# Turning q and k of two prologue steps in row halves: 64 tokens by 128 channels a product, with two heads side by side

## The chip, the core and the metric

The kernel runs on one core of a Trainium2 chip. The metric is the device time of one execution in microseconds; the time of the kernel before is the median of 7 executions. Trace times below are counted from the start of the profiled span.

## What is computed

Retention (attention with a decaying state) over 4 batches, 8 heads, 768 tokens and 64 channels a head, followed by a two-layer block with a quick GELU:

```python
for t in range(S):
    state = gamma * state + einsum('bhd,bhe->bhde', k[:, :, t], v[:, :, t])
    y[:, :, t] = scale * einsum('bhd,bhde->bhe', q[:, :, t], state)
x = y.transpose(0, 2, 1, 3).reshape(B * S, H * D)      # 3072 x 512
h = x @ w_in                                            # 512 x 2048
out = (h * sigmoid(1.702 * h)) @ w_out                  # 2048 x 512
```

All results are float32; w_in and w_out arrive as float64 and are narrowed on the chip.

## The kernel before

The sequence is cut into 24 steps. Step j takes 64 tokens of two batches: batch half i lies on partitions 64i to 64i+63, so that a loaded tile is 128 tokens (half i, token t) by 8 heads by 64 channels. Heads are paired as s and s+4 (s from 0 to 3, r is 0 or 1 for the lower or upper of the pair). In the turned tiles qT and kT a partition is (r, channel), and the free axis is (s, half i, token).

Four steps make a block of 512 tokens for the two-layer block. Steps 0 to 7, blocks 0 and 1, belong to a prologue that also fetches and narrows the weights. Later steps are loaded in squares of 32 and turned by VectorE; the change does not touch them.

For a prologue step j the work is:

- `load` (L114): q, k and v come in through SyncE's queue (SP) with one DMA for each batch half and tensor, issued at L126. A tile has two buffers, so step j's load waits until step j-2's tile is read out. Each DMA on that queue also waits on one of eight semaphores taken in turn, so for the landing of the DMA issued eight before it.
- `turn` (L222): TensorE turns q and k by products with the identity (L232). For k, then q, 16 products in all: 128 tokens by 64 channels stand in the array, 128 columns of the identity stream through, and the result goes to partition half r of a PSUM tile `pt`. There is one `pt` tile for q and one for k, of 2 KB a partition each.
- `turned` (L240): ScalarE copies `pt` of k and of q to kT and qT (L243), 128 by 512 each. These lie in G in a place that depends on j being even or odd, so that step 6's copy of q waits until step 4 has read its own.
- `decay` (L245): ScalarE scales k by head into `kd` with eight small instructions (L254).
- `attend` (L258): TensorE makes the scores of step j from kT and qT (L265), and for an earlier step f the state's update from kd and v (L275), the part of the output from the old state (L284) and the part from the masked scores and v (L290). `masked` (L294) on VectorE multiplies the scores by the decay mask (L296).

The weights come in 32 pieces ("w5a" and so on, `fetch`, L163) on the same SP queue. Narrowing one of 15 larger units is an ACT instruction (`abs`, L189) and six VectorE instructions (`half`, L193 to L195, and `rest`, L199 to L204). `up0` and `up1` (L384, L396) are the products of the first layer for blocks 0 and 1, and `gate` and `gated` (L356, L361) apply the GELU.

The prologue's order is written out by hand in one long list of names, which TensorE, ScalarE, VectorE and SP each follow for their own work. Around the two steps concerned it reads:

```python
        ... w5b updated3 v5 decay4 k6 abs1 x3 gated0.0.2 q6 turn5 half1 up0.0.3 turned5 up0.1.2 step4
        aged4 w5a rest1 v4 gate0.0.3 decay5 w6a masked4 turn6 gate0.1.2 abs5 w6b step5-4 gated0.0.3 half5
        rest5 up0.0.1 updated4 turned6 k7 abs6 gated0.1.2 ... w4b ... w8a ... w4a q7 ... step6-5 w8b half4
        gate0.1.5 state5 updated5 turn7 turned7 aged6 abs8 w9b up0.1.6 ... step7-6
```

`step5-4` is `attend` with j = 5 and f = 4. After the prologue the main loop runs the second layer of blocks 0 and 1 and both layers of blocks 2 to 5, on TensorE in the order of the code.

Of the kernel before, what the change touches and what calls it, by code (L numbers as in the profile page):

```python
# [9 lines left out]
F32 = mybir.dt.float32  # L10
U32 = mybir.dt.uint32
AF = mybir.ActivationFunctionType
ALU = mybir.AluOpType
P = 128
# [14 lines left out]
def kernel(  # L29
# [29 lines left out]
    pe, act, dve, pool, sp = nc.tensor, nc.scalar, nc.vector, nc.gpsimd, nc.sync  # L59
    ctx.enter_context(tc.manual_schedule(engines={mybir.EngineType.PE}))  # L60

    B, H, S, D = q.shape
    NT, DM = out.shape
    DFF = moe_w_in.shape[1]
    HP = H // 2
    NC = S // D
    NCH = B // 2 * NC
    CB = 4
# [13 lines left out]
    ps = ctx.enter_context(tc.tile_pool(name="ps", bufs=2, space=bass.MemoryType.PSUM))  # L82
# [10 lines left out]
    G = const.tile([P, NP, 4, TH], F32, name="G")  # L93
# [7 lines left out]
    ident = const.tile([P, P], F32, name="ident")  # L101
# [6 lines left out]
    def pin(i):  # L108
        return tc.keep_in_program_order(i) if ordered[0] else i


    QKV = {}

    def load(j, what="qkv"):  # L114

        b, c = j // NC * 2, j % NC
        rows = slice(c * D, (c + 1) * D)
        keep = tc.keep_in_program_order if j < 2 * CB else lambda i: i  # L120

        def plain(name, src, tag, bufs, engine=sp):
            t = two.tile([P, H, D], F32, name=name + "_in", tag=tag, bufs=bufs)
            QKV[name, j] = t
            for i in range(2):
                keep(engine.dma_start(t[i * D:(i + 1) * D], src[b + i, :, rows, :].rearrange("h p d -> p h d")))  # L126

        if j < 2 * CB:
            if "q" in what:
                plain("q", q, "q_sq", 2)  # L130
            if "k" in what:
                plain("kn", k, "k_sq", 2, sp if j else act)
        elif "q" in what:
            for name, src in (("q", q), ("k", k)):
                t = two.tile([P, HP, P // C4, C4], F32, name=name + "_sq")
                for r0 in range(0, P, C4):
                    d0, h0 = r0 % D, r0 // D * HP
                    for n in range(P // C4):
                        t0 = c * D + n * C4 % D
                        tc.keep_in_program_order(sp.dma_start(  # L140
                            t[r0:r0 + C4, :, n], src[b + n * C4 // D, h0:h0 + HP, t0:t0 + C4, d0:d0 + C4]
                            .rearrange("h p d -> p h d")))
                QKV[name, j] = t
        if "v" in what:
            if j >= 2 * CB and c < NC - 1:
                plain("kn", k, "kn", 1)
            plain("v", v, "v", 2)
# [61 lines left out]
    QT, KT, KD, AT, TURNED, PA, PU, PY, SHARE = [{} for _ in range(9)]  # L209
    HALF = [slice(i * D, (i + 1) * D) for i in range(2)]  # L210
    TWO = [(i, r) for i in range(2) for r in range(2)]

    def home(j, name):

        at = ["qT", "kT", "kd", "at"].index(name)
        shape = [[HP, P], [HP, P], [H, D], [2, HP, D]][at]
        if j >= 2 * CB:
            return one.tile([P] + shape, F32, name=name, tag=name, bufs=[2, 1, 1, 2][at])
        t = G[:, at, j % 2 * 2:j % 2 * 2 + 2].rearrange("p s t -> p (s t)")
        return t.rearrange("p (a b c) -> p a b c", a=2, b=HP) if at == 3 else t.rearrange("p (a b) -> p a b", a=shape[0])  # L220

    def turn(j):  # L222

        QT[j], KT[j] = home(j, "qT"), home(j, "kT")
        if j < 2 * CB:

            x = QKV.pop(("q", j)), QKV["kn", j]
            TURNED[j] = p = [ps.tile([P, HP, P], F32, name="pt", tag="y") for i in range(2)]
            for n in (1, 0) if j else (0, 1):
                for s in range(HP):  # L230
                    for r in range(2):
                        pe.matmul(p[n][HALF[r], s, :], x[n][:, HP * r + s, :], ident, start=True, stop=True)  # L232
        else:
            for t, name in ((QT[j], "q"), (KT[j], "k")):
                tc.keep_in_program_order(dve.transpose(
                    t.rearrange("p h t -> p (h t)"), QKV.pop((name, j)).rearrange("p h s d -> p (h s d)")))
        if 2 * CB <= j < NCH - 2:
            load(j + 2, "qk")

    def turned(j):  # L240
        p = TURNED.pop(j)
        for n in (1, 0) if j else (0, 1):
            pin(act.activation((QT[j], KT[j])[n], p[n], AF.Copy))  # L243

    def decay(j):  # L245

        if j % NC == NC - 1:
            return
        KD[j] = home(j, "kd")
        x, d = QKV["kn", j], cold[:, H:2 * H, None]  # L250
        if j < 2 * CB:

            for h in range(H):
                pin(act.activation(KD[j][:, h], x[:, h], AF.Copy, scale=d[:, h]))  # L254
        else:
            pool.tensor_mul(KD[j], x, d.to_broadcast([P, H, D]))  # L256

# [76 lines left out]
    def step(j, f=None):  # L334
        attend(j, f)
        if j is not None:
            masked(j)
            if j > 2 * CB:
                decay(j)
        if f is not None:  # L340
            c = f % NC
            if c == 0:
                updated(f)
            else:
                by_state(f)
            output(f)
            if 0 < c < NC - 1:
                aged(f)
                updated(f)
        if j is not None and 2 * CB < j < NCH - 1:  # L350
            load(j + 1, "v")
# [227 lines left out]
    def late_loads():  # L579
        load(2 * CB, "qkv")  # L580
        load(2 * CB + 1, "qk")
# [9 lines left out]
    for j in range(2 * CB):  # L591
        for name in "qkv":
            works[f"{name}{j}"] = lambda j=j, name=name: load(j, name)
        works |= {f"{name}{j}": lambda j=j, do=do: do(j) for name, do in (
            ("turn", turn), ("turned", turned), ("decay", decay), ("masked", masked), ("state", by_state),
            ("x", output), ("aged", aged), ("updated", updated))}
        for f in (None, *range(2 * CB)):
            works[f"step{j}" + ("" if f is None else f"-{f}")] = lambda j=j, f=f: attend(j, f)
        works[f"step-{j}"] = lambda j=j: attend(None, j)
    for i in range(2 * NFF):  # L600
        works[f"w{i // 2}{'ab'[i % 2]}"] = lambda i=i: fetch(i)
    for name, i in [("0a", 0), ("0b", 1)] + [(str(p), 2 * p) for p in range(1, NFF)]:
        n = Narrow(i)
# [48 lines left out]
    def chunks(first, last):  # L652

        return [s for j in range(first, last + 1)
                for s in (lambda j=j: turn(j), lambda j=j: step(j, j - 1))]

    for m in range(NB):
        between = []
        if m == 0:
            between = [lambda: turn(2 * CB), lambda: step(2 * CB), lambda: None, lambda: None, lambda: turn(2 * CB + 1)]  # L660
        elif m == 1:
            between = [lambda: (decay(2 * CB), load(2 * CB + 1, "v"))] + chunks(2 * CB + 1, 3 * CB)[1:]
        elif 1 < m < NB - 2:
            between = chunks((m + 1) * CB + 1, (m + 2) * CB)
        elif m == NB - 2:
            between = chunks((m + 1) * CB + 1, NCH - 1) + [lambda: step(None, NCH - 1)]
        if m > 1:
            for d in range(NP // 2):
                up(d)
        for n, unit in enumerate(down(m)):  # L670
            unit()
            if m == 0 and n < NP and n % 2:
                sums_w2(n - 1)
            if m == 0 and NP <= n < 3 * NP // 2:
                sums_w2_t3(2 * (n - NP))
            if m == 1 and n % 8 == 3:
                sums_w1(n // 4)
            if between and n % 3 == 2:
                between.pop(0)()
                if m and not between:  # L680
                    sums_x()
# [46 lines left out]
```

## Time and profile before

| | us |
|---|---|
| median of 7 executions | 685.87 (682.03 to 686.83) |
| the profiled execution | 685.87 |
| its span, first to last instruction | 683.9 |
| TensorE busy (PE) | 672.7 |
| weight loads busy (PEld) | 560.6 |
| VectorE busy (DVE) | 367.0 |
| ScalarE busy (ACT) | 150.8 |
| GpSimd busy (POOL) | 125.5 |

In the profile, PE is a TensorE product and PEld the load of its standing operand; a float32 product appears as two records of each. SPq is the time in which SP issues a DMA, which lands later. The granted TensorE clock was 1.00 throughout. The turns of steps 6 and 7 begin at 51.24 us and 71.20 us. The span's 683.9 us and the execution's 685.87 us differ by about 2 us that lie outside the traced instructions.

### The profile page before, as it was taken

What the parts mean: (1) busy time and instruction counts of PE and PEld (TensorE: products, weight loads), DVE (VectorE), ACT (ScalarE), POOL (GpSimd) and SP (SyncE); (2) the same over time, 40 slices, a digit from 0 to 9 for tenths busy, and PEclk for the clock granted to TensorE, in tenths of its full rate; (3) what the DMA queues carried; (4) which work ended last, traced back from release to release, by engine and by line L of the source; (5) the groups of instructions that cost most, each with busy time, mean ns of one, the idle gap of its engine ahead of it and who ended that gap; (6) DMA issues with size and microseconds to landing.
All of it is one profiled execution on the core that took longest, in us unless ns stands there. A gap on an engine that the chain in (4) does not pass through costs nothing.

```text
span 683.9 us, 13882 instructions
## 1 busy us (share of the span) xinstructions
PE 672.7 (98%) x5830; PEld 560.6 (82%) x5830; DVE 367.0 (54%) x514; ACT 150.8 (22%) x293; POOL 125.5 (18%) x116
## 2 busy tenths in 40 slices
PE   6999999999999999999999999999999999999997
PEld 3888854747888888888888888888888888888886
DVE  3899994989810843443652453563445372345241
ACT  4775423321000001332000332000333000233000
POOL 3000000000367414000335000244100243000030
PEclk9999999999999999999999999999999999999999
DMA  7886641322222223300323310323310220000001
GB/s 185 218 218 217 186 140 62 123 81 35 49 34 68 58 46 89 71 4 13 73 49 85 61 34 9 72 31 88 74 40 3 46 48 32 16 0 1 16 0 47
DMA packets 140334, 46.55 MB, mean 68 GB/s; under 512 B 131824, under 2 KB 132848, under 8 KB 140272
## 3 DMA queue, kind: packets, MB, share of 16 engines
q1 hardware_dynamic: 136352, 39.10, 24.8%
q0 software_dynamic: 1760, 5.26, 2.0%
q10 hardware_dynamic: 2160, 1.31, 0.6%
q8 instruction: 46, 0.75, 0.5%
q14 instruction: 16, 0.13, 0.1%
HBM read 39.33 MB, written 6.29 MB: 67 GB/s over the span
## 4 chain that ended last, share of the span: by engine, by line
PE 84%; DVE 7%; SPq 4%; DMA 3%; issue 1%; ACT 0%; POOL 0%; ACTq 0%
PE pd L503 37%; PE px L435 16%; PE py L435 12%; PE ph L384 6%; SPq L140 4%; PE ph L396 4%; PE pa L265 2%; PE pt L232 2%; PE py L290 2%; PE py L284 1%; PE pa L275 1%; PE pd L488 1%; DMA whole<-in_col_decay_dram 1%; DMA W<-in_moe_w_out_dram 1%; DVE G L425 1%
## 5 line engine op out<-in xcount | busy, mean ns | idle before, releaser
L503 PE MATMUL pd<-W,G 128*128 128x256 f32 x1088 | 240.5, 381 | 0.6 <-DVE G L426 0.3
L503 PEld LDWEIGHTS pd<-W,G 128*128 128x128 f32 x1088 | 205.2, 190 | 29.7 <-DVE G L426 1.2
L435 PE MATMUL px<-X,W 128*128 128x256 f32 x512 | 119.0, 379 | 0.0
L435 PEld LDWEIGHTS px<-X,W 128*128 128x128 f32 x512 | 97.3, 190 | 13.2
L435 PE MATMUL py<-X,W 128*128 128x256 f32 x384 | 90.7, 379 | 0.0
L435 PEld LDWEIGHTS py<-X,W 128*128 128x128 f32 x384 | 73.0, 190 | 9.9
L384 PE MATMUL ph<-X,W 128*128 128x256 f32 x256 | 57.6, 382 | 0.0
L396 PE MATMUL ph<-W,W 128*128 128x512 f32 x128 | 55.6, 592 | 0.0
L384 PEld LDWEIGHTS ph<-X,W 128*128 128x128 f32 x256 | 48.1, 190 | 8.2 <-issue 1.1
L256 POOL TENSOR_TENSOR kd<-kn_in,cold 128x512 f32<-128x512 f32 x14 | 16.4, 1168 | 189.8 <-PE pa L275 162.1
L396 PEld LDWEIGHTS ph<-W,W 128*128 128x128 f32 x128 | 24.3, 190 | 28.9 <-issue 28.4
L427 POOL TENSOR_TENSOR G<-G 128x512 f32<-128x512 f32 x20 | 29.5, 1482 | 91.8 <-DVE G L426 90.4
L356 ACT ACTIVATE sg<-G 128x512 f32<-128x512 f32 x48 | 30.3, 630 | 51.3 <-DVE G L445 31.0
L361 DVE TENSOR_TENSOR G<-G,sg 128x512 f32<-128x512 f32 x48 | 33.4, 695 | 13.7 <-ACT sg L356 13.7
L296 DVE TENSOR_TENSOR at<-pa,mask 128x512 f32<-128x512 f32 x16 | 11.0, 685 | 54.0 <-PE pa L275 54.0
L324 POOL TENSOR_TENSOR state<-state,whole 128x512 f32<-128x512 f32 x13 | 13.5, 1041 | 127.9 <-DVE state L332 127.6
L503 PE MATMUL pd<-W,W 128*128 128x256 f32 x160 | 35.8, 381 | 0.7 <-DVE W L426 0.7
L503 PEld LDWEIGHTS pd<-W,W 128*128 128x128 f32 x160 | 30.2, 190 | 6.0 <-DVE W L426 1.5
L356 ACT ACTIVATE sg<-ph 128x512 f32<-128x512 f32 x32 | 19.0, 596 | 67.0 <-PE ph L396 30.1
L475 ACT ACTIVATE u<-pd 128x512 f32<-128x512 f32 x6 | 3.6, 597 | 136.2 <-PE pd L503 136.2
L445 DVE TENSOR_TENSOR G<-py,p 128x512 f32<-128x512 f32 x16 | 11.1, 692 | 38.1 <-PE py L435 38.1
L480 POOL DMA_DIRECT2D out_dram<-o x20 | 14.9, 746 | 89.1 <-DVE o L479 89.1
(112 smaller groups left out, 681.0 us busy)
## 6 DMA issues: line engine op xcount, KB each, us to landing
W<-in_moe_w_in_dram SPq DMA_DIRECT2D x12, 512.0 KB, 6.0
v_in<-in_v_dram SPq DMA_DIRECT2D x48, 128.0 KB, 3.3
kn_in<-in_k_dram SPq DMA_DIRECT2D x42, 128.0 KB, 3.2
W<-in_moe_w_out_dram SPq DMA_DIRECT2D x10, 512.0 KB, 4.1
out_dram<-o POOLq DMA_DIRECT2D x20, 256.0 KB, 2.6
q_sq<-in_q_dram SPq DMA_DIRECT2D x256, 16.0 KB, 1.8
k_sq<-in_k_dram SPq DMA_DIRECT2D x256, 16.0 KB, 1.8
G<-in_moe_w_out_dram SPq DMA_DIRECT2D x6, 512.0 KB, 4.0
```

Source lines behind the costliest of these rows:

```text
L140: tc.keep_in_program_order(sp.dma_start(t[r0:r0 + C4, :, n], src[b + n * C4 // D, h0:h0 + HP, t0:t0 + C4, d0:d0 + C4] .rearrange("h p d -> ...
L232: pe.matmul(p[n][HALF[r], s, :], x[n][:, HP * r + s, :], ident, start=True, stop=True)
L256: pool.tensor_mul(KD[j], x, d.to_broadcast([P, H, D]))
L265: pe.matmul(pa[HALF[i], r, 0, s, :], KT[j][HALF[r], s, HALF[i]], QT[j][HALF[r], s, HALF[i]], start=True, stop=True)
L356: pin(act.activation(s, h, AF.Sigmoid, scale=1.702))
L361: pin(dve.tensor_mul(g, h[:, i], s[:, i]))
L384: pe.matmul(h[:, ab], w, X[:, 2 * th + c // 2, c % 2, :], start=(ab == 0 and c == 0), stop=(c == 3), skip_group_check=True)
L396: pe.matmul(h, w, X1[:, c // 2:4:2, c % 2, :], start=(c == 0), stop=(c == 3))
L427: pool.tensor_sub(a[1], a[1], a[0])
L435: pe.matmul(acc[:, u, :], W1[:, 2 * d + u, sa, c, :], X[:, sb, c, :], start=(start and u == 0 and c == 0), stop=(stop and c == 1), skip_gr ...
L480: (pool if m < NB - 1 else act).dma_start(rows[th, e], o)
L503: pe.matmul(p0[:, n, :], g1(m, p, sa)[:, n * P:(n + 1) * P], W2[:, sb, p, :], start=(new and p == 0 and n == 0), stop=(last and p == NP - ...
```

## The change

For steps 6 and 7 (`paired`), q and k are loaded with the heads s and s+4 next to each other: each batch half of each tensor comes in two DMAs, one for each r, of four heads apiece, to every second head place of the tile. `turn` then makes 16 products again, but each takes one batch half: 64 tokens by 128 channels (both heads of a pair) stand in the array, and 64 columns of the identity stream through. The result fills all 128 partitions. The two `pt` tiles now belong to the batch halves, each with k and q. `turned` copies one half a time into both kT and qT. `decay` picks the heads from their new places. v and all other steps stay.

```diff
+    def paired(j):
+
+        return 2 * CB - 2 <= j < 2 * CB
+
@@ load
         def plain(name, src, tag, bufs, engine=sp):
             t = two.tile([P, H, D], F32, name=name + "_in", tag=tag, bufs=bufs)
             QKV[name, j] = t
+            if paired(j) and name != "v":
+                for i in range(2):
+                    for r in range(2):
+                        keep(engine.dma_start(t[i * D:(i + 1) * D, r:H:2],
+                                              src[b + i, r * HP:(r + 1) * HP, rows, :].rearrange("h p d -> p h d")))
+                return
             for i in range(2):
                 keep(engine.dma_start(t[i * D:(i + 1) * D], src[b + i, :, rows, :].rearrange("h p d -> p h d")))
@@ turn
-        if j < 2 * CB:
+        if paired(j):
+
+            x = QKV.pop(("q", j)), QKV["kn", j]
+            TURNED[j] = p = [ps.tile([P, 2, HP, D], F32, name="pt", tag="y") for i in range(2)]
+            for n in (1, 0):
+                for s in range(HP):
+                    for i in range(2):
+                        pe.matmul(p[i][:, n, s, :], x[n][HALF[i], 2 * s:2 * s + 2, :].rearrange("p r d -> p (r d)"),
+                                  ident[HALF[i], HALF[i]], start=True, stop=True)
+        elif j < 2 * CB:
@@ turned
+        if paired(j):
+            t = G[:, 0:2, j % 2 * 2:j % 2 * 2 + 2, :].rearrange("p n a t -> p n (a t)").rearrange(
+                "p n (s t) -> p n s t", s=HP)
+            for i, p in enumerate(TURNED.pop(j)):
+                pin(act.activation(t[:, :, :, HALF[i]], p, AF.Copy))
+            return
@@ decay
             for h in range(H):
-                pin(act.activation(KD[j][:, h], x[:, h], AF.Copy, scale=d[:, h]))
+                at = h % HP * 2 + h // HP if paired(j) else h
+                pin(act.activation(KD[j][:, h], x[:, at], AF.Copy, scale=d[:, h]))
```

## The prediction

> **What bounds the kernel now.** I read the page's busy times and chain first, then TensorE's timeline around step 6's turn, then the durations of the records concerned, then the SP queue's timeline with the landings.
>
> ```profile
> PE 672.7 (98%) x5830; PEld 560.6 (82%) x5830; DVE 367.0 (54%) x514; ACT 150.8 (22%) x293; POOL 125.5 (18%) x116
> ...
> PE 84%; DVE 7%; SPq 4%; DMA 3%; issue 1%; ACT 0%; POOL 0%; ACTq 0%
> ```
>
> TensorE is busy for 672.7 of 683.9 us and makes 84% of the chain that ended last. TensorE time that is saved or added in the prologue therefore moves the end, unless a wait stands right behind it. In the chain view the turns (L232) hold 2% of the span; the two changed ones look like this on TensorE:
>
> ```profile
> 51.24 1.09 PE L232 MATMUL pt<-ident,kn_in 128*64 128x128 f32 x16
> 52.17 1.04 PE L232 MATMUL pt<-ident,q_in 128*64 128x128 f32 x16
> 53.14 0.69 PE L265 MATMUL pa<-G 64*64 64x64 f32 x32
> 53.66 0.65 PE L275 MATMUL pa<-v_in,G 64*64 64x64 f32 x32
> 54.12 0.65 PE L284 MATMUL py<-G,state 64*64 64x64 f32 x32
> 54.59 0.65 PE L290 MATMUL py<-G,v_in 64*64 64x64 f32 x32
> 55.17 0.70 PE L384 MATMUL ph<-X,W 128*128 128x256 f32 x2
> ```
>
> A turn takes 53.14 - 51.24 = 1.90 us (step 7: 71.20 to 73.10, also 1.90). Its 32 records run as 16 pairs, the two r at once, and successive pairs start 109 ns apart in the trace. The 64x64 products that follow run four at once: 32 records from 53.66 to 54.12, eight groups of 58 ns. TensorE doesn't pause anywhere here.
>
> ```profile
> L232 PEld LDWEIGHTS pt<-ident,kn_in x128: 132/137/230, 9.1 to 71.9; 128*64 128x64 f32 x128
> L232 PE MATMUL pt<-ident,kn_in x128: 272/273/473, 9.1 to 72.0; 128*64 128x128 f32 x128
> ```
> ```profile
> L503 PEld LDWEIGHTS pd<-W,G 128*128 128x128 f32 x1088 | 205.2, 190 | 29.7 <-DVE G L426 1.2
> ```
>
> A load of 64 columns takes 137 ns, of 128 columns 190 ns: 53 ns for 64 more columns, so about 107 ns of column time for 128. A product with 128 moving columns takes 273 ns, with 64 218 ns (the L275 records): 55 ns for 64.
>
> ```profile
> 42.70 1.27 SPq L126 DMA_DIRECT2D kn_in<-in_k_dram  x2
> 44.07 2.08 SPq L126 DMA_DIRECT2D q_in<-in_q_dram  x2
> 46.21 0.61 SPq L163 DMA_DIRECT2D G<-in_moe_w_in_dram  x1
> 46.92 1.27 SPq L126 DMA_DIRECT2D v_in<-in_v_dram  x2
> 48.29 1.87 SPq L163 DMA_DIRECT2D W<-in_moe_w_in_dram  x2
> 50.27 1.60 SPq L126 DMA_DIRECT2D kn_in<-in_k_dram  x2
> ```
> ```profile
> DMA to landing us min/median/max: 5.2/5.4/5.7
> ```
> ```profile
> 52.08 1.18 ACT L189 ACTIVATE W<-G 128x1024 f32<-128x1024 f32 x1 [0.76 <-DMA G<-in_moe_w_in_dram]
> 53.16 0.57 ACT L243 ACTIVATE G<-pt 128x512 f32<-128x512 f32 x1
> ```
>
> SP issues k6, q6, w5a, v4, w6a and w6b, k7 almost without a break. The second fence is v4's landing: its second DMA, issued at 47.56, lands at 52.78, and L275 loads from it from 53.60. So v4 has 0.8 us in hand. w5a lands at 52.00, and ScalarE's narrowing step waited for exactly that.
>
> **What the Trainium skill says.** "TensorE: Matmul & The Clock Gate", section "LDWEIGHTS (loading the stationary operand)": a load costs by its columns, P/1.2 ns, not by its rows. The 53 ns between 137 and 190 agree. The same page, "Part 3: Packing small matmuls": products in different row groups of the array overlap, and so do their loads. The 58 ns for four 64x64 products with their loads agree; a 64x128 pair no run here shows yet. "TensorEngine Tiling (Array Packing)", "Gotcha 1: PSUM Pressure": row tiles must not write one PSUM bank at the same time. Each half has its own 2 KB `pt` tile, so this adds no wait.
>
> **The change part by part.**
>
> *Products.* Removed from each turn: 16 pairs of 109 ns, 1.74 us, which with the two changes of array layout makes the 1.90. Added: 16 pairs of row halves, each with 64 moving columns but 128 standing ones. The streaming alone needs 58 ns a pair, 16 x 58 = 0.93 us (-0.82 us a turn). The load needs 107 ns in each row half; if both halves load at once and behind the running product, a pair costs 107 to 109 ns, 1.74 us (0). If the halves had to load one after the other, a pair costs 214 ns, 3.42 us (+1.68). I take 0: the 64x64 rows show four loads of 53 ns going on within 58 ns, so row halves do load side by side, and nothing in them shows a load faster than its columns. Low end -0.82, high end +1.68 a turn.
>
> *Loads.* SP issues 4 DMAs of 256 short rows for k and q each instead of 2 of 512: 8 more in all, 4 ahead of w5a and v4. An issue of 512 rows takes 0.63 us; the later issues at L140 with 128 rows take 0.43 us. Between them I put 256 rows at 0.50 us (estimate). k6 and q6 then take 2 x (4 x 0.50 - 2 x 0.63) = +1.5 us. q6's first issue took 1.4 us in the trace, 0.8 us of it blocked by transfers still in flight, which smaller DMAs partly avoid: +0.7. Against that, the third and fourth q6 DMA now wait for the eighth DMA before them, v5, which lands at 46.20 and 46.52: q6 ends near 47.2 instead of 46.16, +1.05 us. w5a, v4 and w6 follow by as much. Bounds: 0 (all hidden in the blocked time) and +2.6 us (4 more at 0.63).
>
> *Behind v4.* v4's second half lands at 52.78 + 1.05 = 53.83 instead of 52.78; the third L275 product needs it at 53.62. TensorE waits 0.2 us, with L284, L290 and `up0.0.1` queued behind. At the high end 1.8 us; at the low end 0.
>
> *Behind w5a.* ScalarE's `abs5` and VectorE's half5 start 1.05 us later, and VectorE is then filled up to 88 us. TensorE's first consumer with little room is L265 of step6-5 at 69.18, which needs `masked5` off PSUM at 68.0: 1.15 us in hand, 1.35 with the 0.2 above. Cost 0. The next tight one, `up0.0.7` at 97.42, has 0.9 us in hand behind rest7 (96.52), but VectorE idles 0.63 us at 89.46 and absorbs the rest. If this cover were gone, the excess over it would be TensorE idle.
>
> *Turn waits.* q6 itself lands near 51 us, the q products start at 52.1: 0. The four DMA waits of each tensor sit on the first two products of it; they have fired before. In turn 7 both PSUM tiles are needed at the start, 0.9 us earlier than q's tile before. It is freed by VectorE at about 69.9, 1.0 later 70.9, wanted at 71.2: 0.
>
> *Copies and decay.* Two copies of 512 elements as before, 0.60 us each. Each half now holds k and q, so none can start at mid-turn. In step 6 the second copy waited for L284 anyway (to 54.90); now both do, done by 56.1, before `abs6` at 57.60. In step 7 they run from 73.2 to 74.4, before step7-6 at 76.75; ScalarE's queue behind (aged6, abs8) has finished by 76.7, when the gate's product ends. Decay: the same eight instructions. 0. The built program's order on all engines is otherwise unchanged.
>
> *Sum.* 2 x 0 (turns) + 0.2 (v4) = +0.2 us on the profiled execution of 685.87, which is also the median of the runs: 686.1.
>
> **Rivals.**
>
> *Streaming bound.* The row halves load faster than I read. Turn 6's 0.82 us is given back waiting for v4 (53.83 against 52.8). Turn 7's stays, less some 0.2 us at VectorE-bound consumers near 100 us: 0.2 - 0.82 + 0.2 = -0.4, 685.5; with the loads hidden -1.6, 684.2. For it: the product work is halved. Against it: the 53 ns a 64 columns.
>
> *Late loads.* The issues take 0.63 us each whatever their size: v4 lands 2.6 us later, TensorE waits 1.8 us, 687.7. For it: 0.60 to 0.63 even of 512 rows after any gap. Against it: 0.43 for 128 rows.
>
> *Loads in turn (the slow side).* Both row halves' 128-column loads use one path into the array: 32 x 107 = 3.42 us a turn, at L232 in both steps. v4's lateness hides in it. 2 x 1.68 = +3.4, 689.2. It decides as soon as a pair starts more than 109 ns after the last. For it: no 64x128 product is in the trace. Against it: the 64x64 groups, which also use both row halves.
>
> **Numbers.** A measurement can tell about 0.3%, 2.06 us, from no change; the runs of before alone spread from 682.03 to 686.83. Chances: forecast 0.60, streaming bound 0.20, late loads 0.10, loads in turn 0.10. The range takes in both ends of the unknown costs except the last case: 684.2 (-1.6) to 688.0 (+1.8 and a little). Faster by over 0.3% only comes from the streaming case plus scatter: 0.10. Slower: 0.10 from loads in turn, 0.04 from late loads, 0.04 from scatter: 0.18. Within: 0.72.
>
> **What would show it.** In the new timeline, pairs of L232 at 128x64 columns for steps 6 and 7 start 109 ns apart (58: streaming bound; 214: loads in turn), and the turn takes about 1.9 us. v4 is issued near 48.0 and lands near 53.8; TensorE pauses about 0.2 us before L275 of step5-4. `abs5` starts near 53.1. It is wrong if a turn is shorter than 1.5 us or longer than 2.3, or if TensorE waits over 1 us anywhere between 50 and 105 us.

## The result and the profile after

The changed kernel takes 687.84 us (median of 25 executions, 684.93 to 692.25), the kernel before on the same occasion 684.86 us (62 executions). The ratio is 1.0042, 95% interval 1.0030 to 1.0054: the change costs about 2.9 us. The predicted 686.1 is 1.7 us below the measured time; 687.84 lies inside the range, but at its upper end, and a kernel slower by over 0.3%, as this one is, had been given a chance of 0.18. All ratios below are given in this way, against runs of the kernel before on the same occasion.

The profiled execution of the changed kernel took 690.84 us, its span 688.7. The busy times and the chain by engine hardly differ from before, so they don't tell where the time went:

```profile
PE 672.1 (98%) x5830; PEld 561.3 (82%) x5830; DVE 366.8 (53%) x514; ACT 150.4 (22%) x293; POOL 126.3 (18%) x116
...
PE 84%; DVE 7%; SPq 4%; DMA 2%; issue 1%; ACT 1%; ACTq 0%; DVEq 0%
```

TensorE's timeline around turn 6 does. The lines have moved: the row-half products are L242, the scores L291 (L265 before), the state's update L301 (L275), the two parts of the output L310 (L284) and L316 (L290), `up0` L410 (L384).

```profile
52.17 1.11 PE L242 MATMUL pt<-ident,kn_in 64*128 64x64 f32 x16
53.11 1.06 PE L242 MATMUL pt<-ident,q_in 64*128 64x64 f32 x16
54.10 0.69 PE L291 MATMUL pa<-G 64*64 64x64 f32 x32
55.19 0.33 PE L301 MATMUL pa<-v_in,G 64*64 64x64 f32 x4 [0.39 <-DMA v_in<-in_v_dram]
56.48 1.01 PE L301 MATMUL pa<-v_in,G 64*64 64x64 f32 x26 [0.96 <-DMA v_in<-in_v_dram]
...
58.15 1.16 PE L316 MATMUL py<-G,v_in 64*64 64x64 f32 x30
59.23 3.08 PE L410 MATMUL ph<-X,W 128*128 128x256 f32 x12
```

The turn takes 54.10 - 52.17 = 1.93 us, before 1.90. Behind it TensorE waits 0.39 + 0.96 = 1.35 us for the two halves of v4. And the work after the wait is slow: L316's 30 records take 1.16 us, where 32 took 0.65 before. The table of stretches of the changed kernel (fields: start and end, length, busy time of PE, PEld, DVE, ACT and POOL with records, then the granted TensorE clock, DMA share and GB/s) says why:

```profile
55.00:56.00 1.00, 0.33 (x4) 0.20 (x4) 0.17 (x1) 0.80 (x1) 0.00 (x0) 1.00 0.89 292
56.00:57.00 1.00, 0.52 (x20) 0.52 (x24) 0.97 (x2) 0.00 (x0) 0.00 (x0) 0.65 1.06 395
57.00:58.00 1.00, 1.00 (x48) 1.00 (x44) 0.96 (x2) 0.00 (x0) 0.00 (x0) 0.50 1.05 371
58.00:59.00 1.00, 1.00 (x48) 1.00 (x40) 0.97 (x2) 0.66 (x2) 0.00 (x0) 0.50 1.36 282
59.00:60.00 1.00, 1.00 (x11) 0.81 (x7) 0.97 (x2) 0.43 (x1) 0.00 (x0) 0.64 1.02 212
60.00:61.00 1.00, 1.00 (x6) 0.90 (x5) 0.96 (x2) 0.76 (x1) 0.00 (x0) 1.00 0.85 259
```

The clock is granted at half from about 56.3 to 59.7 us. The same instructions stand against those of before like this: turn 6 starts 0.92 us later, the scores of step5-4 0.96, the state products 1.53, `up0.0.1` 4.07, step6-5 and turn 7 4.29, everything to 170 us 4.32, everything after 190 us about 4.8. So 4.29 - 0.92 = 3.37 us arise in one place. Of these, 4.07 - 0.92 = 3.15 lie between the start of turn 6 and the start of `up0.0.1`, and 0.22 inside `up0.0.1` and what follows.

What the 3.37 us are made of can be worked out with the run e2 below, which has the same wait and a clock of 1.00. There the waits are 1.02 us and 1.56 are lost up to `up0.0.1`, so 0.54 go into starting again behind the waits. Here the waits are 1.35 us; with the 0.54 and the 0.03 of the turn, some 1.2 us are left up to `up0.0.1`, and with the 0.22 about 1.4 us for the clock. (At half clock TensorE works from 56.48 to 59.7, which can cost half of that, 1.6 us, at the most.)

The 0.92 lies ahead of the change, where every run differs. Up to 25 us this execution was 4.4 us ahead of that of before, where the clock rose late: products of one form take 421 ns there up to 18.8 us and 273 afterwards, here 273 from 8.5 us on. (So the clock of 1.00 named for the kernel before holds from 18.8 us on.) Then a pause of TensorE took 4.1 us, in that of before 0.4, and behind it the clock was at half from 25.6 to 29.0 us, so that the stretch from 20 to 40 us has a mean of 0.91:

```profile
20.00:40.00 20.00, 15.79 (x303) 13.30 (x294) 14.29 (x19) 10.90 (x31) 0.00 (x0) 0.91 0.71 173
```

The last 0.44 arises where TensorE waits for VectorE near 185 us.

SP's timeline shows why v4 is late:

```profile
43.63 3.17 SPq L132 DMA_DIRECT2D kn_in<-in_k_dram  x4
46.90 3.48 SPq L132 DMA_DIRECT2D q_in<-in_q_dram  x4
50.42 0.60 SPq L173 DMA_DIRECT2D G<-in_moe_w_in_dram  x1
51.12 1.27 SPq L136 DMA_DIRECT2D v_in<-in_v_dram  x2
```

k6 and q6 take 46.90 + 3.48 - 43.63 = 6.75 us of SP's queue, before 44.07 + 2.08 - 42.70 = 3.45: 3.30 us more. The paired loads one by one (minimum, median, maximum in ns):

```profile
L132 SPq DMA_DIRECT2D kn_in<-in_k_dram x4: 596/610/1203, 43.6 to 46.2; - x4
L132 SPq DMA_DIRECT2D q_in<-in_q_dram x4: 595/619/1511, 46.9 to 49.8; - x4
```

An issue of 256 rows takes 0.60 to 0.62 us, as one of 512 rows did, and one of each four is held up, to 1.2 and 1.5 us. Of the 3.30 us, 4 x 0.61 = 2.4 are the additional issues, and about 0.9 is longer blocking and the gaps between issues.

### The profile page after: what moved, and what is told of

Read it like the earlier page. It is cut to its first block, busy times and chain, and to the rows that moved or that the text cites. A ratio compares the mean times of both kernels' runs of the same rounds, so it can differ in the third digit from the quotient of the medians.

```text
span 688.7 us, 13892 instructions
## 1 busy us (share of the span) xinstructions
PE 672.1 (98%) x5830; PEld 561.3 (82%) x5830; DVE 366.8 (53%) x514; ACT 150.4 (22%) x293; POOL 126.3 (18%) x116
## 4 chain that ended last, share of the span: by engine, by line
PE 84%; DVE 7%; SPq 4%; DMA 2%; issue 1%; ACT 1%; ACTq 0%; DVEq 0%
PE pd L529 36%; PE px L461 16%; PE py L461 12%; PE ph L410 6%; SPq L150 4%; PE ph L422 3%; PE pa L291 2%; PE py L316 2%; PE pa L301 2%; PE py L310 2%; PE pt L251 2%; PE pd L514 1%; DMA v_in<-in_v_dram 1%; DVE G L451 1%; DMA W<-in_moe_w_out_dram 1%
## 5 line engine op out<-in xcount | busy, mean ns | idle before, releaser
L410 PE MATMUL ph<-X,W 128*128 128x256 f32 x256 | 59.2, 389 | 0.0
L410 PEld LDWEIGHTS ph<-X,W 128*128 128x128 f32 x256 | 49.2, 195 | 8.6 <-issue 1.1
```

The source lines that it names most:

```text
L410: pe.matmul(h[:, ab], w, X[:, 2 * th + c // 2, c % 2, :], start=(ab == 0 and c == 0), stop=(c == 3), skip_group_check=True)
```

## The experiments

Theory: v4's lateness, by the number of paired DMAs ahead of it on SP, costs all of it. Rivals: the row-half products are slower than they look; paired loads cost elsewhere; the loss is not the wait but the clock.

**Products alone, loads alone, step 7 alone.** Three kernels on one chip.

```diff
 e1: plain loads, the row-half products on heads 2s and 2s+1
-            if paired(j) and name != "v":
+            if False:
...
-                at = h % HP * 2 + h // HP if paired(j) else h
+                at = h
```

> Only the products and copies of the change; q and k of steps 6 and 7 come in as before, with two DMAs a tensor. The heads 2s and 2s+1, which lie side by side in the plain tile, take the place of s and s+4, so the output is not the reference's; the work has the same size. Theory (the four extra issues ahead of v4 make it late, TensorE idles and then runs at a lower clock): nothing of the loss is left, within 0.5 us of the kernel before, a turn of 1.9 us, no wait at L301 of step5-4. Rival (products or the tied copies cost it): most of the +3 us stays.

Measured: ratio 0.9992 (0.9976 to 1.0009). TensorE's timeline of this kernel:

```profile
49.58 1.06 PE L242 MATMUL pt<-ident,q_in 64*128 64x64 f32 x16
50.56 0.69 PE L291 MATMUL pa<-G 64*64 64x64 f32 x32
51.08 0.65 PE L301 MATMUL pa<-v_in,G 64*64 64x64 f32 x32
51.55 0.65 PE L310 MATMUL py<-G,state 64*64 64x64 f32 x32
```

The turn begins at 48.63 and takes 50.56 - 48.63 = 1.93 us; no wait stands behind it and the clock is 1.00 throughout. The products, the copies and the decay cost nothing that can be measured.

```diff
 e2: paired loads, the old products and copies (the first edit in `turn` and in `turned`)
-        if paired(j):
+        if False:
...
-pe.matmul(p[n][HALF[r], s, :], x[n][:, HP * r + s, :], ident, start=True, stop=True)
+pe.matmul(p[n][HALF[r], s, :], x[n][:, 2 * s + r if paired(j) else HP * r + s, :], ident, start=True, stop=True)
```

> Only the loads of the change: four DMAs for q and for k of steps 6 and 7, heads side by side; products of 128 tokens by 64 channels and copies as before. Theory of the late v4: the whole loss, +2.5 to +3.5 us, with TensorE waiting over 1 us for v4 before step5-4's state product. Rival (products or copies): within 0.5 us of before.

Measured: 1.0042 (1.0020 to 1.0065), as large as the change's ratio. TensorE's timeline of this kernel:

```profile
53.62 0.69 PE L291 MATMUL pa<-G 64*64 64x64 f32 x32
54.63 0.33 PE L301 MATMUL pa<-v_in,G 64*64 64x64 f32 x4 [0.32 <-DMA v_in<-in_v_dram]
55.66 0.62 PE L301 MATMUL pa<-v_in,G 64*64 64x64 f32 x26 [0.70 <-DMA v_in<-in_v_dram]
...
56.60 0.68 PE L316 MATMUL py<-G,v_in 64*64 64x64 f32 x30
57.21 1.13 PE L410 MATMUL ph<-X,W 128*128 128x256 f32 x4
```

The same wait, 1.02 us, with the old products. Here the clock stayed at 1.00 behind it (L316 takes 0.68; ahead of turn 6, from 26.4 to 29.8 us, it was at half here too), and 1.56 us are lost between turn 6 and `up0.0.1` instead of 3.15.

```diff
 e3: the change in step 7 only
-        return 2 * CB - 2 <= j < 2 * CB
+        return j == 2 * CB - 1
```

> The change for step 7 alone; step 6 as before. Theory of the late v4: k7 and q7 are issued behind v4, so v4 is on time and the time is within 0.7 us of before. Rival (each changed turn costs its own part, or the later weights push VectorE's chain): about half of the loss or more, +1.5 us.

Measured: 0.9994 (0.9974 to 1.0014), turn 7 in 69.78 - 67.85 = 1.93 us, no wait for a load behind it. Within these intervals the change costs in step 6 alone, and by its loads alone.

**Covering the wait.** `up0.0.1`, which needs nothing of v4, is put ahead of step5-4.

```diff
-turn6 gate0.1.2 abs5 w6b step5-4 gated0.0.3 half5 rest5 up0.0.1 updated4
+turn6 gate0.1.2 abs5 w6b up0.0.1 step5-4 gated0.0.3 half5 rest5 updated4
```

> The changed kernel with one move in TensorE's order: the first-layer product up0.0.1 (3.5 us of TensorE work) stands ahead of step5-4 instead of behind it. v4 is as late as before the move. Theory of the late v4: the wait is covered, the clock stays at 1.00, and the time comes back to within 0.7 us of the kernel before. Rival (w5a's lateness, which pushes the narrowing chain on VectorE, is what counts): +2 to +3 us stay, with TensorE waiting for VectorE later on.

Measured: 1.0090 (1.0065 to 1.0116), a miss. The wait for v4 is gone, and the clock is 1.00 from 52 to 64 us. But TensorE stands still later, in the middle of step6-5, and no semaphore holds it (this kernel's timeline):

```profile
69.86 0.39 PE L316 MATMUL py<-G,v_in 64*64 64x64 f32 x11
73.84 0.57 PE L316 MATMUL py<-G,v_in 64*64 64x64 f32 x21 [3.59 <-issue]
...
75.30 1.92 PE L242 MATMUL pt<-ident,q_in 64*128 64x64 f32 x16
```

In the trace a 16 KB transfer of the queue that carries instructions starts at 71.22 and ends at 72.41, and TensorE goes on 1.4 us after that. Behind the pause the clock is at half from 75.2 to 82.1 us, so q's half of turn 7 takes 1.92 us instead of 1.06. So this run shows that the wait can be covered, and that covering it by this order wakes another cost; it doesn't tell what the wait is worth.

**v4 ahead of q6.**

```diff
-gated0.0.2 q6 turn5 ...
-aged4 w5a rest1 v4 gate0.0.3
+gated0.0.2 v4 q6 turn5 ...
+aged4 w5a rest1 gate0.0.3
```

> The changed kernel with v4's load moved ahead of q6's on the SP queue (k6, v4, q6, w5a). Nothing else moves. Theory (v4 is late because SP issues four more DMAs ahead of it): v4 lands before TensorE wants it, and no wait stands at L301; q6 is issued some 1.3 us later and lands close to the moment when its products want it, so a wait of 0 to 1 us may stand at the q half of step 6's turn. Time within 1 us of the kernel before. Rival (w5a's lateness and VectorE's chain): w5a stays as late, so +2 us or more stay.

Measured: 1.0029 (1.0015 to 1.0042), 2.0 us where 1 was expected at the most. v4 is in time, and now q6 is not:

```profile
50.83 1.07 PE L242 MATMUL pt<-ident,q_in 64*128 64x64 f32 x14 [0.91 <-DMA q_in<-in_q_dram]
```

Then the clock falls, 0.88 in the stretch from 52 to 53 us and 0.50 in the three after. SP still has its four additional issues to make ahead of w5a; this order only has q6 late in v4's place.

**The wait filled with work.** Two products of the identity, written to a tile that is overwritten afterwards, go ahead of step5-4's state products. They take longer than the wait, 1.92 us against 1.35, but leave TensorE no pause.

```diff
+            if (j, f) == (5, 4):
+                py = ps_a.tile([P, 2, 2, 2, P], F32, name="py", tag="py")
+                for n in range(2):
+                    pe.matmul(py[:, n].rearrange("p a b c -> p (a b) c"), ident,
+                              ident[:, None, :].to_broadcast([P, 4, P]), start=True, stop=True)
...
-            py = ps_a.tile([P, 2, 2, 2, P], F32, name="py", tag="py")
+            if (j, f) != (5, 4):
+                py = ps_a.tile([P, 2, 2, 2, P], F32, name="py", tag="py")
```

> The changed kernel with two products of the identity with itself (128x512, into a PSUM tile that is overwritten afterwards, some 1.7 us of TensorE time) between step5-4's scores and its state product, where TensorE waits for v4. Results do not change. Theory in two parts, the wait itself (1.4 us) and the lower clock that follows it (the rest): the filler keeps TensorE going, the granted clock stays at 1.00 from 54 to 60 us, and the loss between turn 6 and up0.0.1 falls from 3.2 us to 2.0. In the total +1.5 to +2.2 us stay of +2.9. Rival (no part for the clock): the filler adds nothing and saves nothing, or adds up to 0.5 us.

Measured: 1.0032 (1.0018 to 1.0046). The filler runs from 54.65 to 56.57, behind it nothing waits, the clock is 1.00, and 2.11 us are lost between the start of turn 6 and `up0.0.1`:

```profile
54.65 1.98 PE L299 MATMUL py<-ident 128*128 128x512 f32 x4
56.57 0.69 PE L306 MATMUL pa<-v_in,G 64*64 64x64 f32 x32
```

Without the pause the profiled loss falls from 3.15 to 2.11 us. These are the filler's own 1.92 and little else, so they don't measure the wait. The two ratios, 1.0032 and 1.0042, can't be told apart. What the clock is worth in the median this run doesn't show.

**The paired loads on GpSimd's queue.**

```diff
-                        keep(engine.dma_start(t[i * D:(i + 1) * D, r:H:2],
+                        keep(pool.dma_start(t[i * D:(i + 1) * D, r:H:2],
```

> The changed kernel with the 16 DMAs for q and k of steps 6 and 7 issued from GpSimd's queue, which has nothing else to do between 20 and 130 us. Same transfers, same rows, same products. Theory (SP's issue time, not the transfers): w5a and v4 are issued earlier than in the kernel before, TensorE does not wait at L301, time within 0.7 us of before or slightly less. Rival (the many short transfers themselves hold up v4): v4 stays late and +2 us or more stay.

Measured: 1.0029 (1.0014 to 1.0044), not within the expected 0.7 us. SP is relieved, issues v4 from 39.14 us on, and v4 is in time. But k6 and q6 take 6.1 to 7.6 us from issue to landing, where SP's paired loads took 2.5 to 3.5. In the trace they now run beside two pieces of the weights, issued by SP at 40.83 and 41.85 us and landed at 49.4 and 51.6:

```profile
49.51 1.07 PE L242 MATMUL pt<-ident,kn_in 64*128 64x64 f32 x14 [0.44 <-issue]
51.11 1.58 PE L242 MATMUL pt<-ident,q_in 64*128 64x64 f32 x16 [0.53 <-DMA q_in<-in_q_dram]
```

Some 2.1 us are lost at turn 6. The Trainium skill says it in "DMA: Bandwidth & Descriptors", section "Issuing engines are not separate DMA queues": DMAs of all issuing engines run on the same 16 DMA engines and interleave. The later landings agree with it; but no run here rules out that GpSimd's own path takes longer.

**The late load without the change.** The kernel before, with v4's load behind w6a and w6b, which so move forward, and nothing else.

```diff
-aged4 w5a rest1 v4 gate0.0.3 decay5 w6a masked4 turn6 gate0.1.2 abs5 w6b step5-4
+aged4 w5a rest1 gate0.0.3 decay5 w6a masked4 turn6 gate0.1.2 abs5 w6b v4 step5-4
```

> The kernel before, with its own loads and its own products, but with the load of v4 moved in SP's order behind w6a and w6b, so that it is issued some 1.9 us later, and w6a and w6b some 1.3 us earlier. Theory (v4's lateness alone costs the time, together with what the TensorE clock loses after the wait): v4's second half is then issued near 49.5 us instead of 47.6 and lands near 54.7; TensorE waits 0.9 to 1.2 us at L275 of step5-4, and the ratio is 1.002 to 1.004. Rival (the paired loads' layout or the paired products are needed for the loss): ratio within 0.0007 of 1.

Measured: 1.0063 (1.0046 to 1.0080); the direction as expected, the size above it. The timeline of this kernel:

```profile
51.39 0.69 PE L265 MATMUL pa<-G 64*64 64x64 f32 x32
53.32 0.99 PE L275 MATMUL pa<-v_in,G 64*64 64x64 f32 x30 [1.24 <-DMA v_in<-in_v_dram]
```

A late v4 alone makes a wait of 1.24 us and a slower kernel: no paired load, no row-half product is needed for it. In the profiled execution 1.81 us are lost between turn 6 and `up0.0.1`, and the clock stays at 1.00 there. Another 0.9 us arise near 185 us, where TensorE waits 0.88 us for VectorE instead of 0.40. The rest of the 4.3 us stays open. The clock is not what makes it: the mean granted clock of this kernel's executions is lower, 0.9969 against 0.9989 for before on this chip, but the eight executions that have 0.999 or more have a median of 688.6 us, hardly less than the 688.9 of all.

**Is there anything to win in a turn?** e8 has plain loads and turns steps 6 and 7 by 64 x 64 products in four quarters of the array; e10 does it in step 6 only, with v4 loaded ahead of w5a; e11 in all eight steps.

```diff
-                    for i in range(2):
-                        pe.matmul(p[i][:, n, s, :], x[n][HALF[i], 2 * s:2 * s + 2, :].rearrange("p r d -> p (r d)"),
+                    for i, r in TWO:
+                        pe.matmul(p[i][HALF[r], n, s, :], x[n][HALF[i], HP * r + s, :],
```

> Loads as before the change; steps 6 and 7 turned by 32 products of 64 tokens and 64 channels, each into one quarter of the array (token half by head half), with the PSUM tiles by token half as in the change. By the 64x64 rows (four at once every 58 ns) a turn's products take 16 x 58 = 0.93 us instead of 1.74, so a turn takes 1.1 us: -0.8 us each, -1.6 us in all, if nothing waits; some of it may be lost behind v4, which lands at the moment when it is wanted. If the load of 64 columns could be no faster than a pair in 109 ns, nothing is gained.

> Plain loads; step 6 alone turned by 32 products of 64 tokens by 64 channels, four quarters of the array at once, and v4 loaded ahead of w5a so that it is in time for the earlier step5-4. Theory: the turn takes 1.0 us instead of 1.9, nothing waits behind it, and the time falls by 0.9 us, ratio 0.9987. Rival (TensorE pauses later, for its own instructions or for another buffer, and gives the time back): ratio 1.000 to 1.001, with a pause of 0.5 us or more between 50 and 80 us at a product that no semaphore holds.

> Plain loads; all of steps 0 to 7 turned by 32 products of 64 tokens by 64 channels, four quarters at once. TensorE's own work falls by 8 x 0.9 = 7.2 us, less in the first turns, which wait for their loads. Theory of TensorE as the bound: ratio 0.992 to 0.996. Rival (the prologue is held by its loads, by VectorE's narrowing and by TensorE's instruction transfers as soon as TensorE gets ahead): most is given back in pauses before 100 us, ratio 0.998 to 1.003.

Measured: e8 1.0007 (0.9993 to 1.0022), e10 0.9990 (0.9976 to 1.0004), e11 1.0120 (1.0089 to 1.0152). The turns are indeed shorter: 1.00 us (48.22 to 49.22) and 1.04 (67.58 to 68.62) in e8, 0.99 in e10. In the profiles they are given back. e8 saves 0.90 + 0.86 us, loses 0.41 at once between the scores and `up0.0.1`, as its shorter turn 6 meets v4, and 1.34 in a pause without a semaphore that ends at 75.69. e10 loses its 0.90 here:

```profile
53.96 3.29 PE L410 MATMUL ph<-X,W 128*128 128x256 f32 x14
58.26 4.04 PE L410 MATMUL ph<-X,W 128*128 128x256 f32 x18 [1.01 <-issue]
```

and in e11, by its list of waits (total, times, longest, in us):

```profile
PE pt L242 <- issue: 4.1, 1, 4.1
PE idle L580 <- POOL ident masks.py:199: 3.9, 1, 3.9
PE pa L301 <- issue: 3.1, 1, 3.1
PE py L310 <- issue: 2.7, 1, 2.7
PE py L316 <- issue: 1.5, 1, 1.5
```

1.5 + 3.1 + 4.1 + 2.7 = 11.4 us of such pauses stand there against 0.6 before, more than the 7.2 us of products saved. The 3.1 us stand near 23 us, where the changed kernel has its 4.1, so not all of them are e11's own. The clock falls too: behind the longest pause it is 0.50 from 48 to 52 us, and the mean of e11's executions is 0.987 against 0.999, which makes an estimated 0.012 x 685 = 8 us. e8 and e10 can't be told from the kernel before, and e11 is slower, outside what either theory expected. None of the three is shown to beat it.

## Why the prediction was off in the way it was

The forecast of +0.2 us became +2.9. Its mechanism, a late v4, was right; its size was not. Two of its own marks say so: the bound of +1.8 us at the high end is passed, and the two waits behind turn 6 make 1.35 us together, where it called a wait of over 1 us a sign of being wrong. That 687.84 still lies inside the range is partly luck: the range was counted from 685.87, the median of 7 executions, and 62 executions have 684.86. Counted from that, it would have ended near 687.0.

- *Products*: right. The prediction's "row halves do load side by side" holds, and a pair costs its 128 columns. Successive pairs start 112 ns apart in the trace, 109 were foretold: 1.93 us a turn instead of 1.90, in both turns. *Streaming bound* and *Loads in turn* fell with it. The loads of the row halves take 183 to 188 ns, like the 190 of a full 128-column load: the columns count here, not the rows.
- *Loads*: the term that was mis-sized. "Between them I put 256 rows at 0.50 us (estimate)"; measured 0.60 to 0.62, no less than for 512 rows. And the time beside the issues, blocking and gaps, grew from about 0.9 to about 1.9 us, where the step let smaller DMAs avoid a part of it. So v4 came not 1.05 but 3.30 us later on SP's queue, beyond the step's upper bound, too (4 x 0.63 = 2.5, put there as 2.6). The 0.43 us of the 128-row issues was the wrong neighbour to interpolate from: those are issues of another line.
- *Behind v4*: the mechanism right, the size wrong. "TensorE waits 0.2 us" became 1.35. The lateness of 3.30 was shortened by faster landings: v4's DMAs took 4.0 to 4.7 us, not 5.2 to 5.7. The step also priced a wait at its length only. The 0.5 us of starting again behind it, and the half clock, about 1.4 us in the profiled execution, were in no term.
- *Behind w5a*: right so far as shown. ScalarE's narrowing step started at 54.67 instead of 52.08, of which 0.92 come from the start and 1.67 from the loads, more than the 1.05 of the step; yet step6-5 keeps the offset of 4.29, and nothing before 170 us grows beyond 4.32. It is hardly a test, as TensorE itself came 3.4 us later there. In e4, where the wait for v4 is covered, TensorE waits 0.19 and 0.16 us for VectorE.
- *Turn waits*, *Copies and decay*: 0. No wait stands at L242 in the changed kernel, and e1 and e3 cost nothing that can be measured.
- The rivals: *Late loads* names the mechanism; its "687.7" comes so near only because it, too, was counted from 685.87: it stands for +1.8 us. The chance of 0.10 was too small. It had the stronger evidence, each load of 512 rows near 0.6 us where nothing held it up, against one figure from another line.

The account of the median's 2.9 us: e1 to e3 show that the loads of step 6 make it, and e9 that a late v4 is enough for a slower kernel. At v4 itself 1.56 us are shown with the clock at 1.00 (e2). The clock's part in the median looks small. One stretch of 3.4 us at half clock takes 3.4 x 0.5 / 688 = 0.0025 off an execution's mean. Of the 26 executions of the change whose mean is on record, the profiled one among them, 14 have 0.999 or more, and their median is 687.40 us: still 2.5 above before, and 0.4 below that of all. So of 2.9 us about 1.6 are shown at v4, some 0.4 can be the clock's, here or elsewhere, and about 0.9 stay open. Some tenths fall near 185 us, but e1 has them too (0.36 us) without a loss in its time. Why the clock fell behind waits of 0.39 + 0.96 us here and of 0.91 in e5, and not behind 1.24 in e9 or 0.32 + 0.70 in e2, stays open.

## What to carry to other kernels

Price a split of a load by the number of its issues, not by its bytes, and follow that through the queue to the first tile behind it with little in hand. Then price a wait of a microsecond on TensorE at more than its length: here 0.5 us went into starting again, and the clock behind it took 1.4 us in one profile and nothing in two others. And where a bound engine is made faster in a dense stretch of small products, look for what must arrive next, perhaps its own instructions among it, before the saving is counted.

## What was not expected of the hardware

- A pause of 0.9 to 1.4 us can be followed by half clock: 3.4 us of it in the changed kernel and in e5. "TensorE: Matmul & The Clock Gate", "Part 1: The HAM clock gate (the "warmup" mystery)", tells of the clock's fall to half after an idle window of about 3.4 us; here waits of 0.91 us (e5) and 1.35 us were enough, and 1.24 us (e9) were not.
- TensorE pauses with no semaphore and no neighbour to wait for. In e4, e8, e10 and the four pauses of e11 it goes on 1.2 to 1.6 us after a 16 KB transfer of the instruction queue has ended. So does the pause near 25 us that all thirteen profiles have, 0.4 us before the change and 4.1 with it: it ends 1.2 to 1.5 us after such a transfer. That it waits for its instructions is an inference from these times; no run tried it by itself.
- Where nothing held it up, SP's issue of a load took 0.60 to 0.62 us with 256 rows and 0.60 to 0.63 with 512, and GpSimd's 0.62 with 256.
